# Four more pieces of key and value loads in an attention decode step, chosen so that the final store is the eighth in the round of the DMA semaphores

## The chip, the cores and the metric

The kernel runs on one core of one Trainium2 chip. The metric is the device time of one execution in microseconds. All times compared here are of fast runs, that is, of runs within 1.5% of the fastest one of the same kernel. A profile covers one execution, and its span is some 2 us shorter than the device time of the same run.

## The reference

A decode step adds an attention branch and a dense branch to the input. The attention uses only the last W = 4096 positions of the caches.

```
x: (2, 1, 448) bf16; k_cache, v_cache: (2, 8, 32768, 256); wq: (448, 4096); wo: (4096, 448)
xn = layernorm(x)
q  = (xn @ wq) as 16 heads of 256
k, v = the last 4096 positions of the caches, each kv head shared by 2 query heads
A  = softmax(q k^T / 16) v, heads joined, @ wo
h  = xn @ w1 + b1                      # w1: (448, 1792)
B  = (h * tanh(softplus(h))) @ w2      # w2: (1792, 448)
out = x + A + B
```

For each of 8 kv heads that is 4 MB of keys and 4 MB of values. With the weights, 77.7 MB have to come in for a result of 1.8 KB.

## The kernel before

All large loads are issued by the sync engine (SP), in the program's order. (The text uses the profile's names: SP; PE, the TensorE matmuls; DVE, VectorE; ACT, ScalarE. A semaphore is a counter that a DMA raises as its data arrives and that an instruction can wait for.) A load of keys or values puts 64 positions of 512 bytes on each of 128 partitions, so that each partition receives one run of 32 KB. `cuts` are the borders of its pieces in positions (T = 64): each piece is a DMA of its own, with a semaphore that its consumers wait for.

```python
    def load_cache(t, cache, i, cuts):
        src = cache[:, i, s0:Sk, :].rearrange("b (p t) d -> p b (t d)", p=PB)
        for lo, hi in zip(cuts, cuts[1:]):
            cols = slice(lo * Dh, hi * Dh)
            nc.sync.dma_start(out=t[:, cols], in_=src[:, :, cols])
    ...
    load_k(0)
    load_dense()
    project()
    ...
    for i in range(Hkv + 1):
        if i + 1 < Hkv:
            load_k(i + 1, (0, T) if i + 1 < Hkv - 1 else (0, T // 2, T))
        if i < Hkv:
            load_v(i, (0, T) if i < Hkv - 1 else (0, T // 2, 13 * T // 16, 15 * T // 16, T))
            load_wo(i, parts=1 if i < Hkv - 1 else 2)
            ... # transposes of k, scores, exp, transposes of p
        ...     # values of head i - 1, its share of the output projection
    res = consts.tile([Bsz, D], BF16)
    ...
    nc.sync.dma_start(out=out.flatten_outer_dims(), in_=res[:])
```

The framework hands out eight DMA semaphores, numbered 0 to 7, in turn to the DMAs in the order of issue. A DMA waits for the one that used its semaphore before it. The keys and the values have two buffers each. At the end of the program SP waits for all eight semaphores, in five instructions of two waits each. In the built program they wait, in this order, for 3 and 2, 4 and 1, 5 and 0, 6 and VectorE, 7 and ScalarE. The before kernel has 36 DMAs; the last of them, the store, has semaphore 3.

The softmax here doesn't subtract the row's maximum and nothing guards it: scores larger than these inputs give would overflow.

Of the kernel before, what the change touches and what calls it, by code (L numbers as in the profile page):

```python
# [34 lines left out]
def kernel(  # L35
# [19 lines left out]
    _, Hkv, Sk, Dh = A_k_cache.shape  # L55
# [7 lines left out]
    T = W // PB  # L63
# [41 lines left out]
    def v_tile():  # L105
        return v_pool.tile([P, T * Dh], BF16, tag="v", name="v")
# [137 lines left out]
    def carry():  # L244
        early = consts.tile([Bsz, D], FP32, name="early")
        nc.vector.tensor_copy(out=early[:], in_=psE[:])
        add_last(ident_f[0:Bsz, 0:Bsz], early[:, :], start=True)
# [55 lines left out]
    def load_dense():  # L303
        w = v_tile()
        dense["w1"] = w[:, 0 : NS * HF].rearrange("p (s n) -> p s n", s=NS)
        nc.sync.dma_start(
            out=dense["w1"],
            in_=B_w1.rearrange("r (x n) -> (r x) n", x=NX).rearrange("(p s) n -> p s n", s=NS),
        )
        dense["w2"] = w[:, NS * HF : NS * HF + NX * NF * D].rearrange(  # L310
            "p (x c d) -> p x c d", x=NX, c=NF
        )
        nc.sync.dma_start(
            out=dense["w2"], in_=B_w2.rearrange("(x q c) d -> q x c d", x=NX, q=P)
        )
# [40 lines left out]
    def dense_out():  # L356
        w2_sb = dense.pop("w2")
        for x in range(NX):
            for c in range(NF):
                add(act_bf[:, c, x, :], w2_sb[:, x, c, :])  # L360
# [7 lines left out]
# [7 lines that stand above are left out]
    def load_k(i, cuts=(0, T)):  # L375
        k_t[i] = k_pool.tile([P, T * Dh], BF16, tag="k", name="k")
        load_cache(k_t[i], A_k_cache, i, cuts)

    def load_v(i, cuts=(0, T)):
        t = v_tile()  # L380
        load_cache(t, A_v_cache, i, cuts)
        v_t[i] = t[:].rearrange("p (t d) -> p t d", t=T)

    def load_wo(kvh, parts=1):
        w = wo_pool.tile([P, rep, ND * D], BF16, tag="wo", name="wo")
        r0 = kvh * rep * Dh
        wo_t[kvh] = w
        if kvh < Hkv - NFIX:

            nc.sync.dma_start(  # L390
                out=w[:].rearrange("p h n -> p (h n)"),
                in_=A_wo[r0 : r0 + rep * Dh, :].rearrange("(p j) d -> p (j d)", p=P),
            )
            return
        win = A_wo[r0 : r0 + rep * Dh, :].rearrange("(h p c) d -> p h (c d)", h=rep, p=P)
        for u in range(parts):
            hs = slice(u * rep // parts, (u + 1) * rep // parts)
            nc.sync.dma_start(out=w[:, hs, :], in_=win[:, hs, :])  # L398

    def turn(s):  # L400
        kt = kt_pool.tile([P, TH * Dh], BF16, tag="kt", name="kt")
        i, half = divmod(s, NH)
        k = k_t[i] if half < NH - 1 else k_t.pop(i)
        nc.vector.transpose(  # L404
            out=kt[:].bitcast(FP32),
            in_=k[:, half * TH * Dh : (half + 1) * TH * Dh].bitcast(FP32),
        )
        kt_t[s] = kt

    def scores(s):  # L410
        i = s // NH
        ktv = kt_t.pop(s)[:].rearrange("p (t n c e) -> p n e t c", t=TH, n=NB, e=NE)
        psc = ps_sc.tile([P, TH, Q], FP32, tag="sc", name="sc")
        for n in range(NB):
            for e in range(NE):
                nc.tensor.matmul(  # L416
                    psc[:],
                    lhsT=qdiag[i % NW][:, n * NE + e, :],
                    rhs=ktv[:, n, e, :, :],
                    start=(n == 0 and e == 0),  # L420
                    stop=(n == NB - 1 and e == NE - 1),
                )
        p_sb = p_pool.tile([P, TH * Q], BF16, tag="p", name="p")
        piece = s % NH
        if piece == 0:
            state["rs", i] = small.tile([P, NH, Bsz], FP32, tag="rs", name="rs")
        pv = p_sb[:].rearrange("p (t c b) -> p b t c", t=TH, b=Bsz)
        sv = psc[:].rearrange("p t (c b) -> p b t c", b=Bsz)
        for b in range(Bsz):
            nc.scalar.activation(  # L430
                out=pv[:, b, :, :],
                in_=sv[:, b, :, :],
                func=ACT.Exp,
                scale=scale,
                bias=off[:, b : b + 1],
                accum_out=state["rs", i][:, piece, b : b + 1],
            )
        p_t[s] = p_sb

    def turn_p(s):  # L440
        pT = p_pool.tile([P, TH * Q], BF16, tag="pT", name="pT", bufs=2 * NH + 1)
        nc.vector.transpose(out=pT[:], in_=p_t.pop(s)[:])  # L442
        pT_t[s] = pT
        i, half = divmod(s, NH)
        if half != NH - 1:
            return
        rs = state.pop(("rs", i))
        total = small.tile([P, 1], FP32, tag="total", name="total")
        nc.vector.tensor_reduce(out=total[:], in_=rs[:], axis=AXIS.XY, op=ALU.add)
        sums = small.tile([P, BR], FP32, tag="sums", name="sums")  # L450
        nc.vector.tensor_scalar(  # L451
            out=sums[:], in0=hsel, scalar1=total[:], scalar2=None, op0=ALU.mult
        )
        state["sums", i] = sums
# [61 lines left out]
    def turn_o(i):  # L516

        o_sb = state.pop(("o", i))
        pq = ps_q.tile([P, NJ * NP * NR], FP32, tag="q", name="q")
        pqv = pq[:].rearrange("p (j u r) -> p j u r", j=NJ, u=NP)  # L520
        for j in range(NJ):
            for u in range(NP):
                nc.tensor.transpose(  # L523
                    pqv[:, j, u, :],
                    o_sb[:, u, j, :, :].rearrange("r h m -> r (h m)"),
                    ident_f[0:NR, 0:NR],
                )
        state["pq", i] = pqv

    def finish(i):  # L530
        pqv = state.pop(("pq", i))
        rec = state.pop(("rec", i))

        o = small.tile([P, NJ, NP, BR], FP32, tag="osum", name="osum")
        for u in range(NP):
            nc.vector.tensor_tensor(
                out=o[:, :, u, :],
                in0=pqv[:, :, u, u * BR : (u + 1) * BR],
                in1=rec[:].unsqueeze(1).to_broadcast([P, NJ, BR]),
                op=ALU.mult,  # L540
            )
        oT = small.tile([P, NJ, Bsz], BF16, tag="oTm", name="oTm")
        with nc.allow_low_precision("sums of fp32 factors, rounded once"):
            nc.vector.tensor_reduce(  # L544
                out=oT[:],
                in_=o[:].rearrange("p j u (b h) -> p j b u h", b=Bsz),
                axis=AXIS.XY,
                op=ALU.add,
            )
        state["oT", i] = oT  # L550
# [38 lines left out]
                    stop=(kvh == Hkv - 1 and h == rep - 1 and c == ND - 1),  # L589
                )  # L590

    load_k(0)
    load_dense()
    project()
    build_q(0)
# [1 line left out]
    turn(0)  # L597
    for i in range(Hkv + 1):
        if i + 1 < Hkv:
            load_k(i + 1, (0, T) if i + 1 < Hkv - 1 else (0, T // 2, T))  # L600
        if i < Hkv:
            load_v(i, (0, T) if i < Hkv - 1 else (0, T // 2, 13 * T // 16, 15 * T // 16, T))
            load_wo(i, parts=1 if i < Hkv - 1 else 2)
            for piece in range(NH):
                s = i * NH + piece
                if s + 1 < NSTEP:
                    turn(s + 1)
                if piece == 1 and i > 1:
                    finish(i - 2)
                scores(s)  # L610
                if i == Hkv - 1 and piece == 2:
                    carry()
                if s >= 1:
                    turn_p(s - 1)
                if s == NSTEP - 1:
                    turn_p(s)
                if piece == 0 and i > 1:
                    turn_o(i - 2)
                if piece == 1 and i > 1:
                    mix(i - 2)  # L620
            if i + 2 < Hkv:
                build_q(i + 2)
        else:
            mix(i - 2)
        if i == 0:
            dense_in()
            dense_out()
        if i >= 1:
            if i - 1 < Hkv - NFIX:
                values(i - 1)  # L630
            else:
                values_fixed(i - 1)
        if i == Hkv:
            mix(i - 1)
# [37 lines left out]
```

## Time and profile before

| | before |
|---|---|
| device time, median of the first 3 runs | 190.11 us (189.6 to 190.15) |
| span of the profiled execution | 187.8 us |
| DMA share from 2.5 to 182.5 us | 1.00 |
| landing of the last load (its last count on the semaphore) | 184.54 us |
| start of the store's issue | 185.59 us |
| from there to the end | 2.25 us |

The page of the profile shows the same in 40 slices of the span (busy share of the DMA engines in tenths, and GB/s), and the share of the load queue below them:

```profile
DMA  6999899999999999999999999999999999999990
GB/s 224 415 479 447 373 432 457 422 447 447 433 433 426 419 415 437 433 433 400 472 445 426 419 433 433 433 433 409 443 443 440 397 423 433 457 443 391 422 378 31
...
q1 hardware_dynamic: 5012, 77.66, 96.9%
```

The row of nines is what matters: between the first slice and the last the DMA engines do not wait for the kernel. (The one 8 comes from the counting: a packet belongs to the slice in which it starts, and the slices on both sides of that one hold 1.03. By the packet records at least 15 packets are under way at every moment from 5 to 182 us.) In such a kernel only three things set the time: when the stream of loads begins, how long it takes, and what follows its end. The swings of single GB/s figures come from counting a packet in one slice; the share is the steadier reading.

### The profile page before, as it was taken

To read this page: it belongs to the slowest core of one execution; us is meant where nothing else is said; L and a number is where in the kernel's file an instruction comes from. 1 tells how busy PE (TensorE), PEld (TensorE's weight loads), DVE (VectorE), ACT (ScalarE), POOL (GpSimd) and SP (SyncE) were. 2 spreads that over 40 slices of the span, in tenths; PEclk is the share of its full clock that TensorE was granted. 3 is DMA by queue.
4 is the path that set the end of the run, shared out by engine and by line. 5 is a ranking of instruction groups with operands and counts; after the bars stand their busy time and mean duration, and the time that the engine had idled before them with its cause. 6 is when DMAs were issued, how large, how long until landed. Compare 5 with 4: busy or idle time off the path is not lost.

```text
span 187.8 us, 2412 instructions
## 1 busy us (share of the span) xinstructions
PE 141.0 (75%) x938; PEld 65.0 (35%) x938; DVE 108.6 (58%) x150; ACT 45.3 (24%) x148; POOL 16.3 (9%) x74
## 2 busy tenths in 40 slices
PE   0397098904989989956896769955995779999682
PEld 0132033801334334422342324321441324444581
DVE  6703597049671994079804991099506993995201
ACT  3003115200152244024222224033302332244001
POOL 7000600300003001100030003000110000000000
PEclk9999759955899999999999999999999999999955
DMA  6999899999999999999999999999999999999990
GB/s 224 415 479 447 373 432 457 422 447 447 433 433 426 419 415 437 433 433 400 472 445 426 419 433 433 433 433 409 443 443 440 397 423 433 457 443 391 422 378 31
DMA packets 5030, 77.81 MB, mean 414 GB/s; under 512 B 534, under 2 KB 1052, under 8 KB 2332
## 3 DMA queue, kind: packets, MB, share of 16 engines
q1 hardware_dynamic: 5012, 77.66, 96.9%
q8 instruction: 7, 0.11, 0.2%
q14 instruction: 3, 0.02, 0.0%
q10 hardware_dynamic: 8, 0.01, 0.0%
HBM read 77.67 MB, written 0.00 MB: 413 GB/s over the span
## 4 chain that ended last, share of the span: by engine, by line
DMA 66%; DVE 20%; PE 8%; SPq 2%; ACT 1%; issue 1%; ACTq 0%; DVEq 0%
DMA k<-in_A_k_cache_dram 57%; DVE kt L404 16%; DMA wo<-in_A_wo_dram 9%; PE sc L416 4%; PE o L484 4%; DVE pT L442 3%; SPq L373 2%; ACT p L430 1%; PE psE L217 0%; SPq L114 0%; DVE sums L451 0%; SPq L398 0%; DVE oTm L544 0%; DVE recm L476 0%; PE psA L234 0%
## 5 line engine op out<-in xcount | busy, mean ns | idle before, releaser
L404 DVE STREAM_TRANSPOSE kt<-k 128x2048 f32<-128x2048 f32 x32 | 73.3, 2296 | 51.1 <-DMA k<-in_A_k_cache_dram 51.1
L416 PE MATMUL sc<-kt,qdiag 128*128 128x512 bf16 x256 | 62.1, 387 | 18.8 <-DVE kt L404 18.1
L430 ACT ACTIVATE p<-sc,off 128x256 bf16<-128x256 f32 x64 | 33.0, 542 | 68.4 <-PE sc L416 67.8
L484 PE MATMUL o<-v,pT 128*8 128x512 bf16 x192 | 42.5, 379 | 0.0
L416 PEld LDWEIGHTS <-qdiag 128*128 128x128 bf16 x256 | 22.9, 97 | 54.4 <-issue 16.5
L484 PEld LDWEIGHTS <-pT 128*8 128x8 bf16 x192 | 17.2, 92 | 22.4
L442 DVE STREAM_TRANSPOSE pT<-p 128x512 bf16<-128x512 bf16 x32 | 21.8, 682 | 4.7 <-ACT p L430 4.7
L286 POOL COPY qdiag<-qt 32x16 bf16<-32x16 bf16 x64 | 12.9, 247 | 120.2 <-PE sc L416 103.0
L493 ACT COPY o_sb<-o 8x512 f32<-8x512 f32 x12 | 6.3, 572 | 36.3 <-PE o L484 36.3
L430 ACT ACTIVATION_READ_ACCUMULATOR p<-sc,off 128x1 f32 x64 | 11.6, 182 | 0.0
L217 PE MATMUL psE<-wo,oTm 128*2 128x448 bf16 x24 | 5.5, 351 | 7.2 <-DVE oTm L544 7.2
L266 PE MATMUL q_ps<-v,xq 128*128 128x512 bf16 x28 | 8.7, 487 | 2.1 <-DVE xq L257 2.1
L217 PE MATMUL psE<-v,act_bf 128*2 128x448 bf16 x14 | 4.4, 493 | 7.0 <-DVE act_bf L354 7.0
L563 PE MATMUL q<-pT,v 128*128 128x4 bf16 x256 | 7.8, 169 | 2.5 <-DMA v<-in_A_v_cache_dram 2.3
L563 PEld LDWEIGHTS <-v 128*128 128x128 bf16 x256 | 7.5, 101 | 3.3 <-DMA v<-in_A_v_cache_dram 3.3
L276 DVE CAST q_sb<-q_ps 128x512 bf16<-128x512 f32 x2 | 1.3, 686 | 8.2 <-PE q_ps L266 8.2
L266 PEld LDWEIGHTS <-xq 128*128 128x128 bf16 x28 | 3.3, 121 | 7.5 <-issue 3.3
L217 PEld LDWEIGHTS <-oTm 128*2 128x2 bf16 x24 | 1.5, 82 | 11.3 <-DVE oTm L544 9.7
L217 PEld LDWEIGHTS <-act_bf 128*2 128x2 bf16 x14 | 1.4, 108 | 9.7 <-DVE act_bf L354 7.1
L190 PE MATMUL xnT_ps<-ident,xn_bf 2*128 2x2 bf16 x7 | 0.5, 166 | 5.7 <-DVE xn_bf L138 5.7
L523 PEld LDWEIGHTS q<-ident_f,o_sb 8*128 8x128 f32 x48 | 3.4, 136 | 2.5 <-issue 2.5
L276 ACT CAST q_sb<-q_ps 128x512 bf16<-128x512 f32 x2 | 1.1, 588 | 12.5 <-PE q_ps L266 12.5
(60 smaller groups left out, 49.5 us busy)
## 6 DMA issues: line engine op xcount, KB each, us to landing
k<-in_A_k_cache_dram SPq DMA_DIRECT2D x7, 4096.0 KB, 27.6
v<-in_A_v_cache_dram SPq DMA_DIRECT2D x7, 4096.0 KB, 29.6
k<-in_A_k_cache_dram SPq DMA_DIRECT2D x2, 2048.0 KB, 24.6
v<-in_B_w_dram SPq DMA_DIRECT2D x2, 1568.0 KB, 24.5
wo<-in_A_wo_dram SPq DMA_DIRECT2D x7, 448.0 KB, 30.2
v<-in_A_wq_dram SPq DMA_DIRECT2D x1, 2048.0 KB, 7.4
v<-in_A_v_cache_dram SPq DMA_DIRECT2D x1, 2048.0 KB, 15.2
v<-in_A_wq_dram SPq DMA_DIRECT2D x1, 1536.0 KB
```

Source lines behind the costliest of these rows:

```text
L217: nc.tensor.matmul(psE[:], lhsT=lhsT, rhs=w, start=start, stop=stop, skip_group_check=True)
L266: nc.tensor.matmul(ps[u][:], lhsT=xq[:, s, :, :].rearrange("p j k -> p (j k)"), rhs=wq_sb[:, s, u * N5 : (u + 1) * N5], start=(s == 0), st ...
L286: nc.gpsimd.tensor_copy(out=tv[rows, :, e, j * Q : (j + 1) * Q : HS].rearrange("p n (b h) -> p n b h", b=Bsz), in_=qv[rows, :, h0 : h0 + r ...
L373: nc.sync.dma_start(out=t[:, cols], in_=src[:, :, cols])
L404: nc.vector.transpose(out=kt[:].bitcast(FP32), in_=k[:, half * TH * Dh : (half + 1) * TH * Dh].bitcast(FP32),)
L416: nc.tensor.matmul(psc[:], lhsT=qdiag[i % NW][:, n * NE + e, :], rhs=ktv[:, n, e, :, :], start=(n == 0 and e == 0), stop=(n == NB - 1 and ...
L430: nc.scalar.activation(out=pv[:, b, :, :], in_=sv[:, b, :, :], func=ACT.Exp, scale=scale, bias=off[:, b : b + 1], accum_out=state["rs", i] ...
L442: nc.vector.transpose(out=pT[:], in_=p_t.pop(s)[:])
L484: nc.tensor.matmul(po[:], lhsT=pT_t[i * NH + piece][:, uh * NP * Q : (uh + 1) * NP * Q : HS], rhs=v[:, u * NP : (u + 1) * NP, :].rearrange ...
L493: nc.scalar.copy(out=o_sb[:, u, :, :, :], in_=po[:, u * Dh : (u + 1) * Dh] .rearrange("r (m j) -> r j m", j=NJ) .unsqueeze(2) .to_broadcas ...
L523: nc.tensor.transpose(pqv[:, j, u, :], o_sb[:, u, j, :, :].rearrange("r h m -> r (h m)"), ident_f[0:NR, 0:NR],)
L563: nc.tensor.matmul(po[:, c, :], lhsT=vv[:, t, c, :], rhs=pTv[:, th, 0:Q:HS], start=(t == 0 and c == 0), stop=(t == T - 1), skip_group_chec ...
```

## The change

Its intent is in the five waits at the end. The store is on semaphore 3, which the first of them waits for, so SP goes through the other four only after the store has landed. With four more DMAs in the program the store is on semaphore 7, in the last of the five. The four DMAs are made by cutting loads of keys and values, in places where a smaller piece also lets its consumer begin earlier.

```diff
-    load_k(0)
+    load_k(0, (0, T // 2, T))
...
-            load_k(i + 1, (0, T) if i + 1 < Hkv - 1 else (0, T // 2, T))
+            load_k(i + 1, (0, T) if i + 1 < Hkv - 1 else range(0, T + 1, T // 4))
         if i < Hkv:
-            load_v(i, (0, T) if i < Hkv - 1 else (0, T // 2, 13 * T // 16, 15 * T // 16, T))
+            cuts = {Hkv - 2: (0, T // 2, T), Hkv - 1: (0, T // 2, 13 * T // 16, 15 * T // 16, T)}
+            load_v(i, cuts.get(i, (0, T)))
```

## The prediction

> **What bounds the kernel now.** I read the stretches first: the span cut by hand into start, three long middles, end of the loads, and tail, with each stretch's busy times and DMA share (last two columns: busy share of the 16 DMA engines, GB/s).
>
> ```profile
> 2.50:60.00 57.50, 37.44 (x186) 17.20 (x187) 30.96 (x49) 11.83 (x38) 7.92 (x34) 0.85 1.01 432
> 60.00:120.00 60.00, 50.48 (x245) 21.33 (x244) 36.50 (x45) 16.02 (x54) 4.90 (x24) 1.00 1.00 430
> 120.00:182.50 62.50, 51.13 (x464) 25.13 (x462) 39.25 (x53) 16.03 (x54) 1.63 (x8) 0.96 1.00 426
> 182.50:184.60 2.10, 1.67 (x49) 1.26 (x47) 0.17 (x1) 0.00 (x0) 0.00 (x0) 0.50 0.38 146
> 184.60:187.80 3.20, 0.34 (x8) 0.08 (x7) 0.53 (x2) 0.49 (x2) 0.00 (x0) 0.50 0.00 1
> ```
>
> From 2.5 to 182.5 us the DMA share is 1.00 (1.01 in the first, where packets of two queues overlap on an engine): the DMA engines are practically never without work, while PE is busy 139 of 180 us and DVE 107. So the loads are the bound, not their waits. Then the chain of work that ended last, its final stretch:
>
> ```profile
> 163.31 0.54 SPq L373
> ...
> 167.20 17.34 DMA wo<-in_A_wo_dram
> 184.54 0.04 issue
> 184.58 0.46 PE psA L234 x8
> 185.04 0.23 ACT res L639
> 185.28 0.27 ACTq L667
> ```
>
> The last piece of wo lands at 184.54 and everything after it is a tail of 187.8 - 184.54 = 3.26 us: 8 matmuls, copies of the result, the store. The chain does not show what follows the store; the view of line 667 (the end of the program) on SP from 186.7 to 187.2 (duration min/median/max in ns, first and last start), and the list of SP's waits do:
>
> ```profile
> L667 SPq EVENT_SEMAPHORE  x5: 27/28/28, 186.8 to 187.0; - x5
> L667 SPq DRAIN  x2: 7/10/13, 187.1 to 187.1; - x2
> ```
>
> ```profile
> SPq L667 <- DMA out_dram<-res: 0.8, 1, 0.8
> ```
>
> SP issues the store at 185.59, waits until it has landed, and only then goes through five waits. In the trace's records they start at 186.759, 186.823, 186.884, 186.949 and 187.010, 63 ns apart, then a drain at 187.075 and two barriers to the end. In the built program these five wait, in order, for DMA semaphore 3, 4, 5, 6, 7 (each paired with 2, 1, 0, DVE, ACT). The store is on 3, the first in the list, so the other four checks, satisfied long ago, stand behind the landing.
>
> **What the Trainium skill says.** (1) "DMA: Bandwidth & Descriptors", section Where 436 GB/s comes from: 16 ports of 27.2 GB/s. The trace agrees: over its packets the median time is bytes / 27.2 GB/s plus 8.1 to 8.7 ns (32,768 B: 1213 ns; 16,384 B: 611; 4096 B: 159; 2048 B: 84). (2) Same page, Why small descriptors are slow, puts a fixed few cycles on each packet; the trace's is those 8 to 9 ns. (3) Same page, Why a DMA increments its semaphore by 16: each engine ends its share with a write to the semaphore; the trace has them as packets of 4 B, 9 ns. (4) "Perfetto Trace Analysis", section Identifying Dependency Chains: instructions with several waits may have EventSemaphore instructions put in before them; that is what the 63 ns steps are.
>
> **The change part by part.** No engine's compute order changes; I compared the built programs, and only SP's list of loads differs, apart from line numbers. Three loads are cut: k of head 0 from one piece of 128 rows of 32 KB to two of 16 KB; k of head 7 from two pieces to four of 8 KB rows; v of head 6 from one to two. Bytes are the same. Four more DMAs move the round of eight on by four: the store goes from semaphore 3 to 7.
>
> *Tail, removed.* The list at the end is the same five waits in the same order, but only the last now waits for the store. The other four run while the store is in flight: it has 1.17 us from issue to its wait's end, four checks need 0.25. Saved: 187.010 - 186.759 = **0.25 us**, on the path, as nothing else is busy there.
>
> *Stream, added.* Each engine moves 8 of 128 rows. k0: 8 packets of 1213 become 16 of 611, +9 x 8 = 72 ns. v6: the same, +72. k7: 16 of 611 become 32 of 8192 B; three such packets on another queue, alone, took 309, so 2 x 309 - 611 = 7, x 16 = +112. Four more semaphore writes at 9 = +36. Sum **+0.29 us** per engine, and as no engine has idle time, the last landing moves from 184.54 to about 184.83.
>
> *SP issue, added.* Four more issues of 0.54 to 0.61 us: 2.3 us of SP, hidden, because SP sits in waits for most of the span (53.2 us on PE at line 373, 51.3 on DVE) and the stream has a transfer of 4 MB (9.7 us) queued behind the running one at each of these places.
>
> *Compute, moved.* k0's first half lands some 4.8 us earlier (4 MB take about 9.7 us), so the first score work can start when q's diagonal tiles are ready; k7's quarters and v6's halves also let their consumers start earlier. The buffer of k0 comes free earlier than 31.49, so k2 is issued earlier; it then waits behind k1 (landed 40.0) and v0 (48.3). v7's issue at 163.31 hangs on the values matmuls of head 5 (PE o, line 484), which no cut touches. None of it makes the stream shorter: worth 0.
>
> Sum: 190.11 + 0.29 - 0.25 = 190.15, and I say **190.1 us**: no net gain to be seen. I give the tail and the stream equal trust.
>
> **The rivals.**
> (a) *A new wait holds SP and the stream runs dry.* With the shifted round, each issue also waits for the DMA eight before it. I matched the new waits with the landings of before: the second half of v6 needs k6 (landed 142.41, while v6 is issued at 142.60: no wait); wo6 needs v5 (landed 152.09), so SP stands there some 9 us, but k7 and v6, 8 MB, are queued; the last wo piece needs v6's first half, by my estimate halfway between 162.84 and 172.51, so 167.7 against its issue at 167.20 now: half a microsecond late with over 15 us of queue ahead of it. For it: these waits are real. Against: never under one transfer in the queue. If wrong, each microsecond of dry queue is a microsecond of time: 191 or more.
> (b) *The earlier start is worth something.* The first scores wait for k (DVE from 21.48), so the intent could be a head start of about 2 us, as q's tiles are there at 21.3 anyway. That pays only if compute were the bound somewhere later; a DMA share of 1.00 in all three middles speaks against. If right, 188 to 189.
> (c) *Smaller pieces cost nothing*, because engines overlap the packet overhead. Then only the 0.25 stays: 189.86. Against: packets of before already stand back to back at bytes/27.2 plus 8.5.
> (d) *Skew between engines.* The last wo piece's shares land between 182.60 and 184.54, so some engines run out 1.9 us before the slowest; part of this comes from seven instruction fetches of 16 KB (0.9 us each on an engine). Where these fall may move the last landing by a few tenths either way; nothing in the change steers it.
>
> **Range and chances.** The three runs of before span 189.6 to 190.15, that is 0.55 us, larger than either of my terms. With (c) and (d) below and (a) above I take 189.4 to 190.9. Two per cent is 3.8 us; the tail that the change touches is 3.26 us in all and the stream is full, so faster by over 2% needs an effect I cannot find (0.01), slower needs a dry queue of 3.8 us (0.01).
>
> **What the profile after would show.** Right, if: the five end waits of SP now straddle the store, four of them starting within about 0.7 us of the start of its issue (which takes 0.33) and only one after it has landed; the time from the store's issue to the end is shorter by 0.2 to 0.3 us (2.2 now); the last wo piece lands 0.2 to 0.4 later than 184.54; DMA share stays 1.00 in the middle stretches; the DVE transposes of k0 start before 21.48 with no effect on the end. Wrong, if: a middle stretch has a share under 0.99 (a dry queue, rival a), the last landing comes earlier than 184.4 (b, c or d), or the end waits keep standing behind the store.

## The result

The changed kernel took 189.76 us (median of 6 runs, 189.52 to 190.06) against 189.89 for the kernel before (6 runs, 189.6 to 190.15). The ratio is 0.9994, with a 95% interval of 0.9979 to 1.0009: the same time. Ratios here are the mean time of one kernel's fast runs over that of the other's of the same rounds, so not quite the ratio of the medians quoted. The interval of 0.0015 to either side is 0.29 us; both of the effects at issue are of that size, and the traces have to tell them apart.

The stretches of the changed kernel (the columns as in the prediction: the stretch, its length, busy us of PE, its weight loads, DVE, ACT and GpSimd with their instructions, then PE's clock, the DMA share and GB/s):

```profile
2.50:60.00 57.50, 38.48 (x185) 17.51 (x186) 30.96 (x49) 11.84 (x38) 7.92 (x34) 0.82 1.01 431
60.00:120.00 60.00, 50.26 (x244) 21.26 (x243) 36.49 (x45) 16.01 (x54) 4.90 (x24) 1.00 1.00 430
120.00:182.50 62.50, 50.84 (x454) 24.96 (x453) 39.36 (x53) 16.03 (x54) 1.63 (x8) 0.96 1.00 425
182.50:184.60 2.10, 1.74 (x56) 1.48 (x54) 0.17 (x1) 0.00 (x0) 0.00 (x0) 0.50 0.51 191
```

The stream is as full as before. The row that moved is the last: between 182.5 and 184.6 the DMA engines are busy for 0.51 of the time instead of 0.38, as the loads end later. The chain that ended last, in its final stretch:

```profile
142.97 24.97 DMA v<-in_A_v_cache_dram
167.93 0.02 issue
167.95 16.93 DMA wo<-in_A_wo_dram
184.88 0.04 issue
184.92 0.46 PE psA L234 x8
```

The last load lands at 184.88, 0.34 us later. The chain also shows one of the new waits: the last piece of wo is issued at 167.95, when the first half of the values of head 6 has landed (its semaphore's previous user). In the kernel before it was issued at 167.20. It is in the chain and costs nothing, as the 16.93 us to its landing are spent behind other loads.

SP at the end of the program (line 668), first from 185.9 to 187.05, then from 187.05 to 187.25:

```profile
L668 SPq EVENT_SEMAPHORE  x4: 28/28/28, 186.3 to 186.5; - x4
```

```profile
L668 SPq DRAIN  x2: 7/10/13, 187.2 to 187.2; - x2
L668 SPq EVENT_SEMAPHORE  x1: 28/28/28, 187.1 to 187.1; - x1
```

This is the change at work. The store is issued at 185.93; four of the five checks are done by 186.53, and only the fifth starts when the store has landed (the last count on its semaphore comes at 187.08). From the store's issue to the end it takes 2.00 us instead of 2.25. So the span grew by 0.34 - 0.25 = 0.09 us (187.84 to 187.93), while the six timed runs were 0.11 us faster in the mean. The two do not contradict each other: the landing of the last load scatters, as the experiments show, and so does what lies between span and device time.

### The profile page after: what moved, and what is told of

It is laid out like the page before. It is cut to its first block, busy times and chain, and to the rows that moved or that the text cites. A ratio compares the mean times of both kernels' runs of the same rounds, so it can differ in the third digit from the quotient of the medians.

```text
span 187.9 us, 2415 instructions
## 1 busy us (share of the span) xinstructions
PE 141.9 (76%) x938; PEld 65.3 (35%) x938; DVE 108.7 (58%) x150; ACT 45.3 (24%) x148; POOL 16.3 (9%) x74
## 4 chain that ended last, share of the span: by engine, by line
DMA 71%; DVE 15%; PE 10%; SPq 2%; ACT 1%; issue 1%; ACTq 0%; DVEq 0%
DMA k<-in_A_k_cache_dram 48%; DMA v<-in_A_v_cache_dram 13%; DVE kt L404 11%; DMA wo<-in_A_wo_dram 9%; PE o L484 4%; PE sc L416 3%; PE psE L217 3%; DVE pT L442 2%; SPq L373 1%; ACT p L430 1%; SPq L114 0%; SPq L306 0%; PE psA L234 0%; DVE sums L451 0%; SPq L313 0%
## 5 line engine op out<-in xcount | busy, mean ns | idle before, releaser
L416 PE MATMUL sc<-kt,qdiag 128*128 128x512 bf16 x256 | 63.1, 392 | 16.2 <-DVE kt L404 15.5
```

The costliest lines, as they stand in the source:

```text
L416: nc.tensor.matmul(psc[:], lhsT=qdiag[i % NW][:, n * NE + e, :], rhs=ktv[:, n, e, :, :], start=(n == 0 and e == 0), stop=(n == NB - 1 and ...
```

## The experiments

My theory had two halves. **Tail:** each check that stands behind the store's landing costs 63 ns, so the eighth place saves four of them, 0.25 us. **Stream:** the DMA engines are never idle, so each added packet and each added semaphore write lengthens it, by 0.29 us for the four cuts. The rivals were that smaller pieces cost nothing because their overhead is overlapped, that the new waits let the stream run dry, and that the eighth place is not what shortens the tail.

The table holds what the traces show: when the last piece of wo lands on the slowest of the 16 engines, the mean over the 16, and the time from the store's issue to the end. The mean is the better measure of the stream's length, for a reason given under the first experiment. The last column is not from the traces: the record lists the span of every run, to 0.1 us, and the column compares the mean over a kernel's runs with that of the kernel before in the same rounds (a gap where there was one run, or no list for the kernel before).

| kernel | store on | cuts | slowest landing | mean landing | store to end | mean span, less before's |
|---|---|---|---|---|---|---|
| before | 3 | none | 184.54 | 183.60 | 2.25 |  |
| changed | 7 | k0, v6, k7 | 184.88 | 183.83 | 2.00 |  |
| changed, again | 7 | k0, v6, k7 | 184.57 | 183.81 | 1.99 | -0.05 |
| store moved alone | 7 | none | 184.37 | 183.63 | 1.99 | -0.31 |
| store moved alone, again | 7 | none | 184.54 | 183.57 | 1.98 | -0.25 |
| cuts alone | 3 | k0, v6, k7 | 184.58 | 183.75 | 2.23 | +0.11 |
| store on 0 | 0 | k0, v6, k7 | 184.62 | 183.70 | 2.09 |  |
| store on 6 | 6 | k0, k7 | 184.65 | 183.64 | 2.06 |  |
| quarters | 7 | all but v7 in 4 | 186.34 | 185.50 | 1.99 | +1.67 |
| eighths | 3 | all but v7 in 8 | 189.66 | 188.77 | 2.25 | +5.27 |
| four DMAs fewer | 7 | wq joined | 184.67 | 183.50 | 1.98 | +0.06 |
| four DMAs fewer, again | 7 | wq joined | 184.62 | 183.53 | 1.99 | -0.03 |
| free cuts | 7 | none in k, v | 184.50 | 183.60 | 2.00 | -0.18 |
| free cuts, again | 7 | none in k, v | 184.60 | 183.53 | 1.99 | -0.28 |

Spans are the steadier measure. What lies between the span and the device time ranges from 1.8 to 2.5 us over these runs, whatever the kernel. And the two trace columns account for them: the shift of the mean landing plus the shift of the tail gives the change of the span within about 0.1 us in every row but the two of the four DMAs fewer.

### The store moved alone

The kernel before with four loads of 4 bytes, issued after the second load of keys. They too wait for their semaphores' former users, so the next load of values is issued at 21.57 instead of 17.49; the keys of head 1 are still queued ahead of it and land at 39.74, so the stream does not notice. No load of keys or values is cut. The loads go to tiles that nothing reads; the result is right.

```diff
         if i + 1 < Hkv:
             load_k(i + 1, ...)
+        if i == 0:
+            for u in range(4):
+                pad = consts.tile([1, 2], BF16, name=f"pad{u}")
+                nc.sync.dma_start(out=pad[:, :], in_=A_x.flatten_outer_dims()[0:1, 0:2])
```

> The kernel before with four loads of 4 bytes put in after the second k load: the store moves from semaphore 3 to 7, no k or v load is cut. My theory (a tail of 63 ns per check that stands behind the store, and a stream that pays 8 to 9 ns per packet): from the store's issue to the end 2.00 us instead of 2.25, last wo landing where it was (184.5, give or take 0.3), four of the five end checks before the store's landing, time -0.25 us, ratio to before 0.9987. Rival 1, the tail's gain is not due to the store's place in the round: 2.25 us stay. Rival 2, the tail's gain is real but does not reach the time: ratio 1.000.

Measured: 189.32 us (189.24 to 189.47) against 189.69, ratio 0.9981, interval 0.9968 to 0.9994. SP at the end, from 185.4 to 186.5, then from 186.5 to 186.7, with the store issued at 185.42:

```profile
L671 SPq EVENT_SEMAPHORE  x4: 28/28/28, 185.7 to 185.9; - x4
```

```profile
L671 SPq EVENT_SEMAPHORE  x1: 28/28/28, 186.6 to 186.6; - x1
L671 SPq DRAIN  x1: 13/13/13, 186.6 to 186.6; - x1
```

Four checks before the landing, one after it, without any cut: the place in the round does it, and it reaches the time. The gain was 0.42 us of means (189.77 to 189.35, over all eleven runs of the kernel before), more than 0.26; in the spans it was 0.31. The run was repeated below. Here the slowest engine landed 0.17 us earlier than in the kernel before, while the mean over the engines was the same within 0.04. That is why the mean is used: in the five traces whose key and value loads are cut as in the kernel before and whose wq is in two pieces, it lies within 183.53 to 183.63, and the slowest landing between 184.37 and 184.60.

### The cuts alone

The changed kernel with the same four loads of 4 bytes, so that the round is turned by eight in all and the store is back on semaphore 3.

> The changed kernel with the same four loads of 4 bytes: the cuts stay, the store is back on semaphore 3. My theory: from the store's issue to the end 2.25 us as in the kernel before, last wo landing 0.3 us later than before (about 184.85), time +0.3 us, ratio 1.0016. Rival, smaller pieces cost nothing (packet overhead overlaps): last landing at 184.5, ratio 1.000.

Measured: 190.21 us (189.71 to 190.28) against 189.69, ratio 1.0017, interval 1.0004 to 1.0031. From 186.7 to 187.15, after an issue at 185.62:

```profile
L672 SPq EVENT_SEMAPHORE  x5: 28/28/28, 186.8 to 187.0; - x5
L672 SPq DRAIN  x1: 7/7/7, 187.1 to 187.1; - x1
```

All five checks stand behind the store again, 2.23 us to the end. The cuts by themselves make the kernel slower, in the times and in the spans, and the store moved alone, which has the same four small loads, shows that these are not the cause; the rival by which the cuts cost nothing falls. But the slowest landing, 184.58, was not the 184.85 that I had expected, and the mean landing was 0.15 us later. The sign of the stream term was right and its size was open.

### Quarters

To make the stream's term large, all loads of keys and values but the last were cut in four: 44 more pieces than before, a multiple of eight plus four, so the store is on semaphore 7 again. The edit is shown against the changed kernel.

```diff
-    load_k(0, (0, T // 2, T))
+    load_k(0, range(0, T + 1, T // 4))
...
-            load_k(i + 1, (0, T) if i + 1 < Hkv - 1 else range(0, T + 1, T // 4))
+            load_k(i + 1, range(0, T + 1, T // 4))
...
-            cuts = {Hkv - 2: (0, T // 2, T), Hkv - 1: (0, T // 2, 13 * T // 16, 15 * T // 16, T)}
-            load_v(i, cuts.get(i, (0, T)))
+            cuts = {Hkv - 1: (0, T // 2, 13 * T // 16, 15 * T // 16, T)}
+            load_v(i, cuts.get(i, range(0, T + 1, T // 4)))
```

> All k loads and all v loads but the last in four pieces (44 more pieces than before, the store again on semaphore 7). My theory: 14 loads x (32 x 309 - 8 x 1213 = 184 ns) + 112 for the last k + 44 semaphore writes x 9 = 3.09 us on every engine's stream, tail -0.25: last landing at 187.6, time 192.7, ratio 1.015, DMA share still 1.00 in the middle. Rival 'pieces cost nothing': 189.6, ratio 0.9987. Rival 'the waits on the DMA eight before let the stream run dry': over 193.5, with a DMA share under 0.99 in a middle stretch.

Measured: 191.39 us (191.25 to 191.74) against 189.69, ratio 1.009, interval 1.0076 to 1.0104. The stretches:

```profile
2.50:60.00 57.50, 45.40 (x221) 20.54 (x222) 37.75 (x58) 13.60 (x43) 7.93 (x34) 0.88 1.00 423
60.00:120.00 60.00, 47.76 (x228) 19.90 (x226) 34.17 (x42) 15.31 (x52) 4.89 (x24) 1.00 1.01 426
120.00:182.50 62.50, 49.01 (x412) 23.49 (x412) 34.62 (x48) 14.98 (x52) 1.63 (x8) 0.88 1.01 425
```

The share stayed at 1.00 and above, so nothing ran dry, and the GB/s fell from 432, 430 and 426 in the kernel before to 423, 426 and 425. The pieces do cost, as the theory has it, but less than I had said. The mean landing moved by 1.90 us, not by 3.09. The durations of the packets add up as I had summed them: over the 16 engines those of the load queue are 185.09 us each, 3.10 more than in the kernel before. So durations overlap, which is also how a share can come to 1.01. In the packet records of the traces the most frequent distance from the start of one packet to the start of another of its size shows what a packet takes from the stream:

| bytes of a packet | duration | start to next start | less bytes / 27.2 GB/s |
|---|---|---|---|
| 32,768 | 1213 ns | 1209 or 1210 | 4.7 |
| 16,384 | 611 | 607 or 608 | 4.8 |
| 8,192 | 309 | 306 | 4.8 |
| 4,096 | 159 | 155 or 156 | 4.7 |
| 2,048 | 84 | 80 | 4.7 |

(The last column uses the mean of the pair where there are two, each weighted by how often it occurs: 1209.4, 607.1 and 155.3.) The distances themselves give the 27.2: 28,672 bytes more, from 4 KB to 32 KB, take 1054.1 ns more. The next packet begins 3 to 4 ns before the last one ends. Over the eight packets of a DMA on one engine, from its first start to that of the next DMA, the distance is 9681 ns in the kernel before and 2453 in the quarters: eight steps and 6 ns more, which is what the semaphore write takes, whose record says 9.

By these distances a 4 MB load takes 9681 ns whole, 2 x 4862.4 = 9725 in halves (the distance from one half to the next DMA in the changed kernel), 4 x 2453.2 = 9813 in quarters. The quarters then cost 14 x 132 + (9813 - 9725) for the last keys = 1.94 us. Measured: 1.90. (An expectation below has 9730 for the halves; that is 5 ns too much and changes nothing in the sums to 0.01 us.)

### Eighths

This was a test of the corrected term on a new size, and of the waits: with pieces of 512 KB at most eight DMAs, 4 MB, can be in flight. All loads of the quarters are cut in eight (104 pieces more than before, store on semaphore 3).

> All k loads and all v loads but the last in eight pieces of rows of 4 KB (104 pieces more than before, store on semaphore 3, so no gain in the tail). The quarters moved the last landing by 1.8 us, not by the 3.09 that packet durations gave; in the traces the next packet of an engine starts 3 to 4 ns before the last one ends, so a packet takes bytes/27.2 GB/s + 4.5 ns of the stream, not 8.5. By pitch: 14 loads x 8 x (8 x 155.3 - 1209.4 = 33 ns) = 3.7, k of head 7 0.2, semaphore writes 104 x 4 to 5 ns = 0.5: +4.4 us, 194.1, ratio 1.023. By the durations of my prediction: +7.9 us, 197.6, ratio 1.042. Rival, nearly every load now waits for the DMA eight before it (4 MB in flight) and the stream runs dry: DMA share under 0.99 in a middle stretch, and more than by pitch.

Measured: 194.89 us (194.66 to 195.53) against 189.63, ratio 1.028, interval 1.026 to 1.03. The mean landing moved by 5.17 us. By the distances (155.3 ns a packet, 1248.4 a DMA, 9987 a load) the pieces cost 14 x 306 + 262 = 4.55 us, and by the durations 7.9. The 4.4 that I expected was 0.8 too low, and the remaining 0.6 us lie in one place. Three stretches:

```profile
10.00:20.00 10.00, 7.72 (x26) 2.92 (x24) 2.78 (x4) 2.36 (x3) 0.10 (x1) 1.00 1.00 389
20.00:60.00 40.00, 34.55 (x184) 16.45 (x184) 27.85 (x27) 10.60 (x38) 6.31 (x32) 0.87 1.02 420
60.00:120.00 60.00, 50.48 (x218) 20.55 (x218) 33.38 (x42) 15.30 (x52) 4.89 (x24) 0.91 1.03 419
```

And SP's longest waits:

```profile
SPq L373 <- DMA k<-in_A_k_cache_dram: 44.2, 62, 2.1
SPq L373 <- DMA v<-in_A_v_cache_dram: 33.0, 46, 0.9
```

SP now spends 77 us waiting for earlier DMAs, in 108 waits, and from 10 us on the share is 1.00 or more in each stretch (from 2.5 to 10 it is 0.96, as in the kernel before): the rival of the waits falls even here, as 4 MB in flight are 9.7 us of work. From 20 us on the stream brings the 419 to 420 GB/s that the distances give. From 10 to 20 us it brings 389, which is 0.3 MB less or 0.7 us, and with 4.55 that is the 5.17 measured within 0.15. The packet records put the loss between 11 and 13 us, where the stream passes from wq to the first piece of keys (issued at 1.65, so long queued). Up to four of the engines are without a packet for part of that time, but over all engines that is 0.1 us; in the main, packets of 4 KB take up to 391 ns instead of 159. In the quarters the same passage shows no such thing. What slows these packets is not known; no run here changes that passage alone.

### The store on semaphore 0 and on semaphore 6

Two looks at how the tail grows with the place of the store. The first is the changed kernel with one load of 4 bytes, the second the changed kernel without the cut of the values of head 6.

> The changed kernel with one load of 4 bytes more, so the store moves to semaphore 0, which the third of the five end checks waits for (they wait for 3 and 2, 4 and 1, 5 and 0, 6 and DVE, 7 and ACT). My theory: two checks before the store's landing, the third at 1.16 us after its issue, two behind it; from the store's issue to the end 2.00 + 2 x 0.063 = 2.12 us. Rival, only the eighth place is special or the time depends on how many DMAs there are: 2.25 or 2.00. A single look, its time is not used.

> The changed kernel without the cut of v of head 6: one piece fewer, the store on semaphore 6, which the fourth check waits for. My theory: one check behind the landing, from the store's issue to the end 2.06 us. Rival as for the store on 0. A single look, its time is not used.

Measured: 2.09 us with the store on 0, and 2.06 with it on 6. SP with the store on 0, from 185.9 to 186.2, the store issued at 185.66:

```profile
L672 SPq EVENT_SEMAPHORE  x3: 28/28/705, 186.0 to 186.1; - x3
```

In the records of the first, two checks start before the landing, the third spans it (it starts 0.46 us after the store's issue and lasts 705 ns, as its second wait is the store's), and two follow at 1.200 and 1.262. In the second, three checks start by 0.51 and the fourth at 1.166, with one behind it at 1.228. The tail is 2.00, 2.06, 2.09 and 2.25 us with none, one, two and four checks behind the landing: 63 ns each, but for the store on 0, where the check that spans the landing has begun before it, and the next one starts 36 ns after its end. The eighth place is not special; it is one end of a scale. Nor is the number of DMAs what counts: in the runs with the store on 7 there are 32, 40 or 80 of them and the tail is 1.98 to 2.00, and in those with it on 3 there are 36, 44 or 140 and it is 2.23 to 2.25.

### Four DMAs fewer

The other way round to the eighth place: wq in one piece, and wo of the heads 0 to 5 in three loads of two heads. To make room in SBUF, `xq` was put into the free end of wq's tile, one tile of the dense branch was used twice, and the wo pool has two buffers of two heads.

```diff
-    for lo, hi in ((0, SC), (SC, NS)):
+    for lo, hi in ((0, NS),):
...
-        w = wo_pool.tile([P, rep, ND * D], BF16, tag="wo", name="wo")
+        if kvh % 2 == 0:
+            two = wo_pool.tile([P, 2, rep, ND * D], BF16, tag="wo", name="wo")
+            wo_t[kvh], wo_t[kvh + 1] = two[:, 0, :, :], two[:, 1, :, :]
+        w = wo_t[kvh]
         if kvh < Hkv - NFIX:
+            if kvh % 2 == 0:
+                nc.sync.dma_start(out=..., in_=...)   # rows of both heads
+            return
```

> The other direction: four DMAs fewer than before (wq in one piece, wo of heads 0 to 5 in three loads of two heads), which also puts the store on semaphore 7. My theory: tail 2.00 us; stream shorter by 8 packets (68 ns) and 4 semaphore writes (36 ns), 0.10 us; time -0.35 us, 189.5, ratio 0.998. Rival 'the first queries come later because wq lands whole': PE starts the projection 3 us later; if that counted, +1 us or more. Rival 'pieces cost nothing': -0.25, hardly to be told from mine.

> Four DMAs fewer once more. Its first trace had the tail (1.98 us) and a mean landing 0.10 us earlier, but the last engine landed 0.13 later, and two of six times were over 190.2. If that was chance: ratio 0.998 to 0.999. If the whole wq load costs something that the profiled execution does not show: again 1.000 or more, with some times over 190.2.

Measured: 189.74 us (189.31 to 190.62) against 189.69, ratio 1.0007, interval 0.9987 to 1.0026; again, 189.66 (189.56 to 190.05) against 189.70, ratio 0.9998, interval 0.9986 to 1.0011. The traces show both halves of the theory: 1.98 us of tail, and a mean landing of 183.50 and 183.53, some 0.07 us before that of the five uncut traces. The time did not follow. In both traces the slowest engine lands at 184.62 or later, some 0.1 us after the average of the uncut ones, although the mean is earlier. That takes up part of the 0.3 us expected. The spans say that the loss is real and inside the program: 187.77 us in the mean of the second six against 187.80, where the sum asked for 0.35 less. (In the first six one run has a span of 188.8, 1 us above the others, for a reason not known; no time of the second six is over 190.2, so neither of the two outcomes that I had named for it came.) It is not the later start: the projection begins at 11.9 us instead of 8.7, but the first key transpose at 21.83 and 21.50 against 21.48. In both traces the engines' landings draw apart at one place, from 1.5 us to 2.3, with the first load that lands after an instruction fetch of 16 KB at 69.6 and 69.5; rival (d) below comes back to this. Whether that happens in the runs without a trace too, and so is all of the loss, stays open.

### Free cuts

If the cost of a cut is its packets, a load should be cut where its packets are separate already: x and b1 by row, w2 and wo of head 6, which consist of two runs per partition, by half. That is four more DMAs and no more packets in a key or value load.

```diff
-    nc.scalar.dma_start(out=x_bf[:, :], in_=A_x.flatten_outer_dims())
+    for b in range(Bsz):
+        nc.scalar.dma_start(out=x_bf[b : b + 1, :], in_=A_x.flatten_outer_dims()[b : b + 1, :])
...                                             # b1 in the same way
-        nc.sync.dma_start(out=dense["w2"], in_=...)
+        for x in range(NX):
+            nc.sync.dma_start(out=dense["w2"][:, x, :, :], in_=w2_in[:, x, :, :])
...
-            load_wo(i, parts=1 if i < Hkv - 1 else 2)
+            load_wo(i, parts=1 if i < Hkv - NFIX else 2)
```

> The kernel before with four cuts where the packets were separate already (x and b1 by row, w2 and wo of head 6 by half), so the store is on semaphore 7 and no packet of a k or v load is added. My theory: tail 2.00 us, stream +0.02 us, time -0.23 us, ratio 0.9988. Rival, the cuts themselves cost whatever they cut: ratio 1.000 as for the changed kernel.

Measured: 189.50 us (189.38 to 189.55) against 189.63, ratio 0.9989, interval 0.9975 to 1.0002. The mean landing is 183.60, as before; the tail is 2.00 us.

### All in the same rounds

Then the changed kernel, the free cuts and the store moved alone were run once more on one chip, with shared runs of the kernel before.

> The changed kernel once more, in the same rounds as the three below. By start-to-start times (a load of 4 MB takes 9681 ns of an engine whole, 9730 in two pieces, 9813 in four) its stream is 49 + 49 + 83 = 181 ns longer, its tail 0.25 us shorter: -0.07 us, ratio 0.9996. Mean landing of the last wo piece 0.15 to 0.25 later than before. By the term of my prediction (0.29) it would be +0.04, ratio 1.0002: the two are not told apart by the time, only by the landing.

> The four free cuts once more, against the changed kernel in the same rounds: tail 2.00 us, mean landing as before, ratio to before 0.9988 and 0.15 to 0.2 us faster than the changed kernel. Rival, no difference between where the cuts are: the same time as the changed kernel within 0.05 us.

> Four loads of 4 bytes once more: as the free cuts, ratio 0.9988. Its first ratio of 0.9981 had about 0.1 us more than the 0.25 of the tail; if that is chance of where the slowest engine lands (184.37 against a mean landing equal to before), it is gone now.

| | median us | range | ratio to before | 95% interval | mean span |
|---|---|---|---|---|---|
| before | 189.70 | 189.56 to 190.11 | | | 187.80 |
| changed | 189.55 | 189.44 to 190.13 | 0.9996 | 0.9982 to 1.0010 | 187.75 |
| free cuts | 189.45 | 189.34 to 189.69 | 0.9983 | 0.9971 to 0.9995 | 187.52 |
| store moved alone | 189.42 | 189.38 to 189.97 | 0.9987 | 0.9974 to 0.9999 | 187.55 |

The free cuts' end, from 185.9 to 187.0, with the store issued at 185.65:

```profile
L670 SPq EVENT_SEMAPHORE  x5: 28/28/28, 186.0 to 186.8; - x5
L670 SPq DRAIN  x2: 7/7/7, 186.9 to 186.9; - x2
```

The first four checks start from 185.93 to 186.12 and the fifth at 186.71: they straddle the store, where five behind it take 0.25. The four measurements with the store on semaphore 7 and no added packets in the keys and values gave 0.9981, 0.9989, 0.9983 and 0.9987; their mean, 0.9985, is 0.28 us, and the tail gives 0.26. The free cuts are 0.21 us of means (189.67 to 189.46) faster than the changed kernel in these rounds. By the times alone that would be inside the noise (an interval from the two spreads is 0.28 to either side), but the spans differ by 0.23 with 0.16 to either side. It is the size that the cuts' term of 0.18 us asks for. The free cuts are the version that I would keep, though all of this is a seventh of a per cent.

## Why the prediction was right or wrong

The time, the range and the class were right: 189.76 us lies in 189.4 to 190.9, and 190.1 is 0.3 us above. Of that, 0.22 was the starting point, the median of three runs (190.11; of six it was 189.89), and 0.1 the term for the stream. That the range held is no proof of its steps: it is 1.5 us wide, several times either term. By its own steps:

- **The stream is the bound.** Right: the share stayed 1.00 in all three middle stretches, and each added packet showed in the mean landing.
- **Tail, -0.25 us.** Right in mechanism and size: 2.254 to 2.000 us in the two traces. The store moved alone shows that it comes from the place in the round, and the looks at 0 and 6 show the scale.
- **Stream, +0.29 us.** This step was mis-sized. Durations of packets were added, and they overlap by 3 to 4 ns each. The prediction held against rival (c) that packets stand back to back at their bytes plus 8.5 ns; from start to start it is bytes plus 4.7 to 4.8. A possible sign of it was on the page: the share of 1.01 in the first stretch, which the prediction put down to packets of two queues, is the load queue's own (1.007; the others add 0.001). By start-to-start times the terms are 44 ns for k of head 0, 44 for v of head 6 and 88 for k of head 7, semaphore writes included: 0.18 us. The four traces with all these cuts have a mean landing of 183.77 against 183.59 for the five without, which is 0.18. The last landing of the profiled execution, 0.34 later, seemed to confirm the larger figure; the repeat landed at 184.57.
- **The sum, +0.04.** With the term corrected it is 0.18 - 0.25 = -0.07 us, a ratio of 0.9996. Measured: 0.9994 and 0.9996, each within 0.0015. That the changed kernel is faster at all is inside the noise.
- **SP issue hidden, compute moved for nothing.** Right. The first key transpose starts at 19.51 instead of 21.48 and the load of k of head 2 is issued at 29.48 instead of 31.49; that load lands at 60.40, where it landed at 60.41 before. (The prediction has v of head 0 landing at 48.3 ahead of it; it was 49.69, which changes nothing.) Rival (b) was worth nothing.
- **Rival (a).** The new waits came where the prediction had them: SP waits 8.0 us for the values of head 5 before it issues wo of head 6, and the last wo piece waits for half of v of head 6, which landed at 167.93 (predicted: 167.7). The stream was not thinner, and even the eighths with their 108 waits kept the share at 1.00 or more from 10 us on.
- **Rival (c).** It falls with the cuts alone and the quarters, though a part of it is true: nearly half of what a packet's duration has above its bytes is overlapped with the next packet.
- **Rival (d).** It was named and underrated. The slowest engine's landing differs by up to 0.31 us between two traces of the same kernel, as much as either term; my test "the last wo piece lands 0.2 to 0.4 later" could not be read off one trace. The traces also show where the engines draw apart, which I had not looked at. In all fourteen the landings of one load lie within 1 us of each other until a first instruction fetch of 16 KB at 34 to 38 us, and those of the next load to land after it has ended are 1.7 us apart or more. In the changed kernel's first trace the distance grows again, from 1.8 to 2.4, with the load that lands after the fetch at 68.6; in the repeat it does not. No run moved a fetch, so this is read and not tested.

## What to carry to other kernels

In a kernel whose loads never pause, sum what you change in two places only, the stream and what follows it, and take the cost of a packet from start to start, not from its duration. Waits that are satisfied early cost nothing here before the last landing and 63 ns each behind it, so the last transfer should be what the last wait waits for; turn the round with cuts where the runs are separate already. When the effects are smaller than the scatter of the times, make one of them ten times larger, or read both in the traces and the spans of several kernels.

## What the Trainium skill lacked or had wrong

- "DMA: Bandwidth & Descriptors", Why small descriptors are slow: that section gives a fixed cost per packet in cycles and no measured time. Here it was 4.7 to 4.8 ns of an engine's stream for packets of 2 to 32 KB; the records' durations show 8 to 9, of which 3 to 4 overlap with the next packet.
- The same page, Anatomy of one DMA, calls the semaphore write's bubble about one cycle, in its account of DMAs issued from GpSimd. Here, issued from SP, each DMA's write took 6 ns of an engine's stream (9 by its record).
- The same page, Measured, has 341 GB/s for 1 MB, issued from GpSimd. In this stream, which is issued from SP and never empty, 1 MB pieces came to 423 to 426 GB/s and pieces of 512 KB to about 420, against 426 to 432 in the kernel before: the table's figure is not what pieces of that size reach when they queue behind each other.
- "Perfetto Trace Analysis", Identifying Dependency Chains, tells of added EventSemaphore instructions, not of their cost: 61 to 70 ns from one to the next on SP when their semaphores are already there.
- No page that I read says that the order of the waits at the program's end decides how many of them stand behind the last store: 0.25 us here, between the first place and the last.
